# Layer 1 of tokens 0-1023: blocks 7 to 10 in seven products, GpSimd emptied, signs by parametric ReLU, running sums in PSUM, other planner margins

## The chip, the core and the metric

One Trainium2 core runs the whole program. The metric is the device time of one execution in microseconds (us), the median of the runs. PE is the matrix engine, DVE the vector engine, ACT the scalar engine, POOL is GpSimd, SP issues the DMAs.

## What is computed

```python
x = attention(q, k, v)          # 4 x 8 heads, 576 x 64; half local (32 wide), half strided (32)
x = x / rms(x) * rms_g          # 2304 tokens x 512
h = silu(x @ w_gate) * (x @ w_val)            # d_ff 1536 = 12 blocks of 128
x = h @ w_out                                 # layer 1
h = softplus(x @ w_in)                        # d_ff 2048 = 16 blocks of 128
out = h @ w_out2                              # layer 2
```

Weights come as 64-bit floats and are turned into 32-bit floats on the chip.

## The kernel before, in words

**Products.** Each operand of a product is split in a high and a low part (`split_op`, `prep_in`, `prep_out`: ACT rounds the high part, DVE subtracts it), and each product is three matmuls (`mm3`, L459). Tokens lie in chunks of 512. Chunks 0 and 1 (tokens 0-1023) are "side 0" of layer 1, the others "side 1".

**Plain and in seven products.** `plain` makes one 128 x 512 result of gate or value with 12 matmuls. A block of d_ff over two chunks has four such results, 48 matmuls. `quad` makes the same four by Strassen's scheme (Winograd's form): seven products of 6 matmuls each, 42 in all. For it the token operands B11 to B22 (tile `ob`) are joined by four sums T1 to T4 (tile `tb`, made by `combine`), the weights by four sums (`prep_in` with `sums`), and partial results are copied and added (ACT L919 and L926, DVE L923). Before the change side 0 uses `plain` in all 12 blocks; side 1 and layer 2 use `quad`.

**Output of layer 1.** For every two blocks `out1` multiplies by w_out: six matmuls into a PSUM bank, then DVE adds the bank to the running sum `xs` (L1007).

**Weights.** `decode` makes a 32-bit float from a 64-bit one: ACT scales the upper word (L392), ACT or DVE fetches the low bits (L393 or L395), DVE takes the sign in with one operation (L397) and joins with a second (L400). 74 tiles are decoded; 42 are also written back to `w_kept` for the second use.

**Order.** Nothing runs in the order it is written. `Program.add` records an operation with its engine, its estimated length and its dependencies; `Program.emit` plays it through (`Trial`), and issues on every engine in the order of that trial. It does so twice: the first pass holds the attention and the first `DEALT` = 10 blocks of side 0, whose products fill PE beside the second half of the attention (a step of the attention queue after each product); the second pass holds all that follows. Operations made by `two` may go to POOL, if DVE has over `BESIDE` = 900 ns of work at that point.

**At the seam** the second pass makes the last norms (`last_turn`: L488 to L493), blocks 10 and 11 of side 0, and, with `combine` and `build`, the operands of side 1.

Of the kernel before, what the change touches and what calls it, by code (L numbers as in the profile page):

```python
# [37 lines left out]
W1N, W2N = DFF // 128, DF2 // 128  # L38
DEALT = 10
HOMES = (4, 6, 12)  # L40
# [4 lines left out]
WARM = 9  # L45
BESIDE = 900
EXTRA = {"gh": 3, "gl": 3}
# [5 lines left out]

HOP = {"PE": 210, "DVE": 175, "ACT": 240, "POOL": 90, "SP": 60}
WINDOW = 3413
SLACK = 10
# [5 lines left out]
class Program:  # L62
# [70 lines left out]
    def hop(self, e, i):  # L133
        return 0 if e == "PE" == self.nodes[i][0] else HOP[e]


class Trial:
# [20 lines left out]
    def run(self):  # L158
# [48 lines left out]
        while len(ends) < len(new):  # L207
# [52 lines left out]
def attn_glu_softplus(  # L260
# [17 lines left out]
    def all_of(key):  # L278
        return (key, 0, 1 << 30)
# [23 lines left out]
    def table(name):  # L303
        pr.add("ACT", 1300, lambda: nc.scalar.preload_act_table_set(name), [], [all_of("table")])

# [36 lines left out]
    x_banks = [(banks.t[i], (f"bank{i}", 0, 1 << 20)) for i in (2, 3)]  # L342
    raws = ring(const, "raw", 2, [128, 512], U64)
    cvt = ring(const, "cvt", 1, [128, 512])
# [39 lines left out]
    def decode(src, t, kt, keep):  # L384

        raw, kraw = raws.next()
        u, ku = cvu.next()
        words = raw.bitcast(U32).rearrange("p (n two) -> p n two", two=2)
        wlo, whi = words[:, :, 0], words[:, :, 1]
        quarters = raw.bitcast(U16).rearrange("p (n four) -> p n four", four=4)  # L390
        dma(340, lambda: nc.sync.dma_start(out=raw, in_=src), hold, [kraw])
        act(512, lambda: nc.scalar.activation(t, whi.bitcast(F32), AF.Copy, scale=2.0 ** -112), [kraw], [kt])  # L392
        pr.add("ACT", 180 + 512 / 0.98, lambda: nc.scalar.activation(  # L393
            u, quarters[:, :, 1], AF.Identity, bias=low, scale=2.0 ** -13), [kraw, all_of("eps")], [ku], alt=(68 + 512 / 1.5,
            lambda: nc.vector.tensor_scalar(out=u, in0=wlo, scalar1=29, scalar2=None,  # L395
                                            op0=ALU.logical_shift_right)))
# [3 lines left out]
        dve(560, lambda: nc.vector.scalar_tensor_tensor(  # L400
            out=t.bitcast(U32), in0=t.bitcast(U32), scalar=3, in1=u,
            op0=ALU.logical_shift_left, op1=ALU.bitwise_or), [kt, ku], [kt])
        if keep >= 3 * AGAIN:
            dma(170, lambda: nc.sync.dma_start(out=wk[keep], in_=t), [kt], [("wk", keep, keep + 1)])
# [60 lines left out]
    def stats(c, ring_):  # L465
        lo, hi = CUTS[c], CUTS[c + 1]
        n = hi - lo
        r, kr = sview(lo, hi), ("ssq", lo, hi)
        p, kp = ring_.next()
        p = p[:, :n]  # L470
        for i, kk in enumerate((0, 2, 1, 3) if c < 2 else (0,)):
# [398 lines left out]

    def step(queue, n=1):
# [24 lines left out]
    def plain(i, row, c, ring_):  # L896

        bank = ring_.next()
        lo, hi = (A11, A12) if row == 0 else (A21, A22)
        if c == 4:  # L900
            terms = [(a, B12, k, ((2 * j + k) // 2, (2 * j + k) % 2 * 256)) for j, a in enumerate((lo, hi)) for k in (0, 1)]
        else:
            xlo, xhi = (B11, B21) if c % 2 == 0 else (B12, B22)
            terms = [(a, x, k, None) for a, x in ((lo, xlo), (hi, xhi)) for k in (0, 1)]
        n = CUTS[c + 1] - CUTS[c]
        prod(bank, i, terms, n)
        return bank[0][:, :n], bank[1]
# [83 lines left out]
    def out1(fs, g, first, c, d):  # L991
# [5 lines left out]
        for f in fs:  # L997
            i = f % 4
            mv, km = g[f, c]
            pairs.append(([wout[i][:, x, d * 128:(d + 1) * 128] for x in (0, 1)], mv,  # L1000
                          lambda a, b, i=i, km=km: [(f"wout{i}", a * 512 + d * 128, a * 512 + d * 128 + 128), km[b]]))
        mm3(pb, kp, pairs, n)
        x, kx = xview(d, lo, hi)
        if first:
# [32 lines left out]
    def combine(c0, c1, over):  # L1037

        for k in (0, 1):
# [11 lines left out]
            split_op(y, ky, T4, k, eng="DVE")  # L1051

    def build(c0, c1, c4, sums=True):

# [11 lines left out]
    def w_at(f, side):  # L1066
        return (f % 2, 0) if side else (0, f % 2 * 4)

    def prep1(f, side, parts=(0, 1)):
        src = [None] * 3 if side and f >= AGAIN else [w1[f, :, j * 512:(j + 1) * 512] for j in range(3)]  # L1070
        if 0 in parts:
            prep_in(w_at(f, side), [(3 * f, src[0]), (3 * f + 1, src[1])], side, True, "POOL")
        if 1 in parts:
            prep_out(f % 4, 3 * f + 2, src[2])
# [5 lines left out]
    def prep2(p, all4, eng):  # L1080
        i = ((W1N + p) % 2, 0)
        o = 3 * W1N + 4 * p
        prep_in(i, [(o, None), (o + 2, None)], True, all4, eng)
        for j in (0, 1):
            prep_out((2 * p + j) % 4, o + 2 * j + 1, None)
        return i

    with tc.manual_schedule():
# [29 lines left out]
        def early():  # L1118
            use.s = s_banks
            direct(0)  # L1120
            half(0, 0, f_banks)
            stats(0, v_banks)

# [48 lines left out]
        with ExitStack() as c2:  # L1172
# [3 lines left out]
            pr.side = True  # L1176
            half(1, 0, s_banks)
            pr.side = False
            table("silu_and_others")
# [13 lines left out]
            for i in (0, 1):  # L1193
# [5 lines left out]
                fk["gv"].t.append(ssq[:, i * CH:i * CH + CH])  # L1199
            queue, last_turn = steps(x, {-1: (1,), 1: (2,)}, tv)  # L1200
            step(queue, 5)
# [4 lines left out]
            prep1(DEALT, 0)  # L1206
            pr.emit()
            if RAW:
                fk["gv"].t, fk["gv"].keys = fk["gv"].t[:2], {}
                give(i for i in (0, 1) if i not in RAW)  # L1210
# [19 lines left out]
        for s, f in enumerate([*range(AGAIN, W1N), *range(AGAIN)]):  # L1230
# [15 lines left out]
            g[f, c1] = chain1(gb1, vb1)  # L1246
            for k in range(max(0, 3 * s - 6), min(3 * s - 3, 2 * W1N)):
                early2(k)
# [6 lines left out]
        for side, (c0, c1, c4) in enumerate(SIDES):  # L1255
# [97 lines left out]
```

## Time and profile before

| | |
|---|---|
| median of 3 runs | 895.45 us (894.0 to 895.78) |
| the profiled execution | 895.19 us |
| its span, first to last instruction | 893.4 us |
| PE busy | 877.4 us (98%), 5372 instructions |
| DVE busy | 699.6 us (78%), 1291 |
| ACT busy | 508.3 us (57%), 977 |
| POOL busy | 61.5 us (7%), 57 |

The busy time of an engine is the union of its instructions' durations. On DVE the duration of an instruction runs a little into that of the next one, so instructions that follow each other at once start closer than they last. Of PE's matmuls some records are missing.

### The profile page before, as it was taken

What the parts mean: (1) busy time and instruction counts of PE and PEld (TensorE: products, weight loads), DVE (VectorE), ACT (ScalarE), POOL (GpSimd) and SP (SyncE); (2) the same over time, 40 slices, a digit from 0 to 9 for tenths busy, and PEclk for the clock granted to TensorE, in tenths of its full rate; (3) what the DMA queues carried; (4) which work ended last, traced back from release to release, by engine and by line L of the source; (5) the groups of instructions that cost most, each with busy time, mean ns of one, the idle gap of its engine ahead of it and who ended that gap; (6) DMA issues with size and microseconds to landing.
All of it is one profiled execution on the core that took longest, in us unless ns stands there. A gap on an engine that the chain in (4) does not pass through costs nothing.

```text
span 893.4 us, 14068 instructions
## 1 busy us (share of the span) xinstructions
PE 877.4 (98%) x5372; PEld 726.9 (81%) x5372; DVE 699.6 (78%) x1291; ACT 508.3 (57%) x977; POOL 61.5 (7%) x57
## 2 busy tenths in 40 slices
PE   7999999999999999999999999999999999999998
PEld 6677887888877888888888888888888888888887
DVE  4999999997699976787998798867798456666545
ACT  2997766663454677464665468644474655434331
POOL 1010202110013100000100010000010000000000
PEclk7999999999999999999999999999999999999999
DMA  7765766522211454453542024511114011101003
GB/s 245 251 200 165 248 218 211 166 99 105 71 59 48 132 182 158 154 195 123 188 135 79 1 96 153 172 52 48 48 48 165 24 48 48 48 27 44 1 1 118
DMA packets 41141, 102.17 MB, mean 114 GB/s; under 512 B 4721, under 2 KB 5745, under 8 KB 41073
## 3 DMA queue, kind: packets, MB, share of 16 engines
q1 hardware_dynamic: 41072, 101.27, 35.0%
q8 instruction: 42, 0.69, 0.3%
q14 instruction: 27, 0.21, 0.1%
HBM read 80.28 MB, written 20.97 MB: 113 GB/s over the span
## 4 chain that ended last, share of the span: by engine, by line
PE 89%; DVE 6%; ACT 3%; DMA 2%; issue 1%; SPq 0%; DVEq 0%
PE bank L459 84%; PE bank L760 1%; PE bank L706 1%; PE bank L617 1%; DVE xs L1007 1%; DMA id_sb<-ident 1%; DMA w_kept<-cvtx 1%; DVE xs L376 1%; DVE tb L376 1%; DVE gv L376 0%; PE bank L483 0%; ACT eb L664 0%; PE bank L604 0%; ACT eb L668 0%; DVE gv L492 0%
## 5 line engine op out<-in xcount | busy, mean ns | idle before, releaser
L459 PE MATMUL bank<-ob,win 128*128 128x512 f32 (+1 forms) x1560 | 441.3, 360 | 1.2 <-ACT win L430 0.7
L459 PEld LDWEIGHTS bank<-ob,win 128*128 128x128 f32 x1560 | 282.6, 188 | 54.5 <-issue 2.3
L459 PE MATMUL bank<-tb,win 128*128 128x512 f32 x672 | 233.2, 392 | 1.4 <-DVE xs L1007 1.2
L459 PEld LDWEIGHTS bank<-tb,win 128*128 128x128 f32 x672 | 124.3, 188 | 24.3 <-DVE xs L1007 1.4
L1029 DVE TENSOR_TENSOR xs<-bank,xs 128x512 f32<-128x512 f32 (+1 forms) x127 | 86.8, 685 | 52.4 <-PE bank L459 51.1
L430 ACT ACTIVATE win<-w 128x512 fp32r<-128x512 f32 (+1 forms) x136 | 83.4, 615 | 54.9 <-PE bank L459 28.7
L376 DVE TENSOR_TENSOR win<-w,win 128x512 fp32r<-128x512 f32 (+1 forms) x125 | 84.3, 678 | 22.3 <-ACT win L430 19.4
L459 PE MATMUL bank<-wout,ghx 128*128 128x512 f32 x304 | 99.7, 389 | 0.0
L459 PE MATMUL bank<-wout,gh 128*128 128x512 f32 (+1 forms) x276 | 89.9, 386 | 0.0
L459 PE MATMUL bank<-ghx,wout 128*128 128x512 f32 x224 | 84.1, 393 | 0.0
L459 PE MATMUL bank<-gh,wout 128*128 128x512 f32 (+1 forms) x256 | 80.1, 353 | 1.4 <-DVE xs L1007 1.1
L1007 DVE TENSOR_TENSOR xs<-bank,xs 128x512 f32<-128x512 f32 (+1 forms) x100 | 62.4, 630 | 11.0 <-PE bank L459 9.6
L459 PEld LDWEIGHTS bank<-wout,ghx 128*128 128x128 f32 x304 | 56.9, 188 | 11.8
L459 PEld LDWEIGHTS bank<-wout,gh 128*128 128x128 f32 x276 | 51.2, 188 | 10.6
L459 PE MATMUL bank<-wout,glx 128*128 128x512 f32 x152 | 53.8, 389 | 0.0
L459 PEld LDWEIGHTS bank<-gh,wout 128*128 128x128 f32 x256 | 45.3, 189 | 10.1 <-DVE xs L1007 2.5
L459 PEld LDWEIGHTS bank<-ghx,wout 128*128 128x128 f32 x224 | 42.0, 188 | 8.4
L459 PE MATMUL bank<-wout,gl 128*128 128x512 f32 (+1 forms) x138 | 48.1, 386 | 0.0
L376 DVE TENSOR_TENSOR w<-w 128x256 f32<-128x256 f32 x110 | 46.0, 418 | 1.1
L459 PE MATMUL bank<-glx,wout 128*128 128x512 f32 x112 | 43.4, 394 | 0.0
L459 PE MATMUL bank<-gl,wout 128*128 128x512 f32 (+1 forms) x128 | 42.4, 351 | 0.0
L393 ACT ACTIVATE cvu<-raw,low 128x512 uint32<-128x512 uint16 x44 | 33.6, 763 | 11.4 <-DVE cvtx L400 4.5
(164 smaller groups left out, 1234.2 us busy)
## 6 DMA issues: line engine op xcount, KB each, us to landing
raw<-w SPq DMA_DIRECT2D x74, 512.0 KB, 3.8
w<-w_kept SPq DMA_DIRECT2D x52, 256.0 KB, 2.6
qk<-qk SPq DMA_DIRECT2D x15, 608.0 KB, 6.8
w_kept<-cvtx SPq DMA_DIRECT2D x25, 256.0 KB, 2.5
cvt<-w_kept SPq DMA_DIRECT2D x25, 256.0 KB, 2.8
w_kept<-w SPq DMA_DIRECT2D x20, 256.0 KB, 2.8
w_kept<-cvt SPq DMA_DIRECT2D x17, 256.0 KB, 2.5
cvtx<-w_kept SPq DMA_DIRECT2D x17, 256.0 KB, 2.8
```

Of the source, the lines that this page charges most:

```text
L376: pr.add("DVE", 68 + n / 0.96, lambda: getattr(nc.vector, name)(o, x, y), r, w, alt=(110 + n * 2.3, lambda: getattr(nc.gpsimd, name)(o, x, ...
L393: pr.add("ACT", 180 + 512 / 0.98, lambda: nc.scalar.activation(u, quarters[:, :, 1], AF.Identity, bias=low, scale=2.0 ** -13), [kraw, all_ ...
L430: act(n, lambda: nc.scalar.activation(h, t, AF.Copy), [kt], [reg(0, o + lo, o + hi)])
L459: lambda a=a, b=b, i=i, st=st, mv=mv: nc.tensor.matmul(o, lhsT=st[a], rhs=mv[b], start=(first and i == 0), stop=(last and i == m - 1), ski ...
L617: nc.tensor.matmul(sp[o, a * nk:(a + 1) * nk], lhsT=qt[r, c:c + 64], rhs=qt[r, QW + c:QW + c + nk], start=False, stop=True, skip_group_che ...
L706: pr.add("PE", 108, lambda a=a, a0=a0, tp=tp: nc.tensor.transpose(tp[:kp, a * 128:a * 128 + 128], pv[:, a0 + a, :], id_sb), [kpv, all_of(" ...
L760: pr.add("PE", 59 if loc else 36, lambda a=a, h=h, o=o, t=t: nc.tensor.matmul(xb[64 * h:64 * h + 64, a * nq:(a + 1) * nq], lhsT=vt[r0:r1, ...
L1007: dve(n, lambda: nc.vector.tensor_add(x, pb, x), [kp, kx], [kx])
L1029: dve(n, lambda x=x, pb=pb: nc.vector.tensor_add(x, pb, x), [kp, kx], [kx])
```

## The change

It does five things.
1. **Blocks 7 to 10 of side 0 by `quad`** (`QUADS`, `side_q`). `combine_ops` makes T1 to T4 for side 0 out of the split operands, since `xs` holds the running sums by then; `combine` for side 1 moves from block 10 to block 11. `DEALT` goes to 5, and the attention queue takes three steps at a time (`PACE`).
2. **Nothing on GpSimd** (`BESIDE` = 1e9): 51 tensor operations go from POOL to DVE. Two memsets stay.
3. **Signs by parametric ReLU**: ACT scales the upper word with another factor for negative numbers (`Prelu`, alpha -2^32), so that the sign is in the exponent and comes out of the shift; the first of the two joining operations on DVE goes.
4. **Running sums copied into PSUM** (`KEPT`): on side 0, from the second pair of blocks on, ACT copies `xs` into the bank ahead of `out1`'s matmuls, these add onto it, and the bank is copied back by ACT or DVE. 36 additions on DVE become 36 copies in on ACT and 36 copies out (23 on ACT, 13 on DVE).
5. **Margins**: in the planner a result for PE counts as 100 ns later, and a DMA's as 1600 ns later for the others. A third buffer `raw`; four more buffers `gvw`; `early2` (decoding for layer 2) all in side 1 of layer 1.

```diff
-DEALT = 10
+DEALT, QUADS = 5, (7, 11)
+PACE = 3
+KEPT = (0, 1, 2, 3)
+KEEPF = 2
-BESIDE = 900
+BESIDE = 1e9
+MARGIN, LATE = 100, 1600
+def lag(e, to):
+    if e == "PE":
+        return 0 if to == "PE" else HOP[e]
+    return HOP[e] + (MARGIN if to == "PE" else LATE if e == "SP" else 0)
...
-        act(512, lambda: nc.scalar.activation(t, whi.bitcast(F32), AF.Copy, scale=2.0 ** -112), [kraw], [kt])
+        act(512, lambda: nc.scalar.activation(t, whi.bitcast(F32), AF.Prelu, scale=2.0 ** -112, alpha=-2.0 ** 32),
+            [kraw, all_of("slope")], [kt])
+            shifted.append(nc.vector.tensor_scalar(out=u, in0=ti, scalar1=3, scalar2=None, op0=ALU.logical_shift_left))
+            a, b, n, op = (wlo, u, 29, ALU.logical_shift_right) if shifted else (ti, u, 3, ALU.logical_shift_left)
+            nc.vector.scalar_tensor_tensor(out=ti, in0=a, scalar=n, in1=b, op0=op, op1=ALU.bitwise_or)
-        dve(560, lambda: nc.vector.scalar_tensor_tensor(
-            out=u, in0=t.bitcast(U32), scalar=0x80000000, in1=u, op0=ALU.bitwise_and, op1=ALU.bitwise_or),
-            [kt, ku], [ku])
...
+        if c < 2 and d in KEPT and fs[0] >= KEEPF and kp[0] in primed:
+            act(n, lambda: nc.scalar.activation(pb, x, AF.Copy), [kx], [kp])
+            mm3(pb, kp, pairs, n, False)
+            evict(n, x, pb, [kp], [kx])
+            return
...
+    def combine_ops():
+        for k in (0, 1):
+            y = whole(B12, k)
+            t = fk["gv"].next()
+            less(t, y, parts(B11, k))
+            split_op(*t, T1, k, eng="DVE")
+            z = whole(B22, k)
+            less(y, z, [y])
+            split_op(*y, T3, k, eng="DVE")
+            less(z, z, [t])
+            split_op(*z, T2, k, eng="DVE")
+            x = whole(B21, k)
+            less(x, x, [z])
+            split_op(*x, T4, k, eng="DVE")
...
+            if f in range(*QUADS):
+                if f == QUADS[0]:
+                    drain(len(todo))
+                    o_banks.t, o_banks.keys = banks.t[4:], {}
+                side_q(f)
+                continue
             side_a(f, [None, None, (last_turn,)] if f == DEALT else [])
             if f == DEALT:
+                combine_ops()
+            if f == QUADS[1]:
                 combine(*SIDES[1][:2], False)
```

**How the order moves.** The first pass holds 1,545 matmuls and 429 operations on DVE before, 1,191 and 344 after; the program has 24 matmuls fewer in all (1,752 of 512 columns with `ob` or `tb` before, 1,728 after).

DVE, just behind the seam, before (`gv` and `tb`: sums for side 1; L1007: additions of `out1`; L397 and L400: a decode):

```order
L1007 TENSOR_TENSOR xs<-bank_76,xs 128x512
L376 TENSOR_TENSOR gv_84<-xs,gv_85 128x512
L376 TENSOR_TENSOR tb<-gv_85,tb 128x512
L1007 TENSOR_TENSOR xs<-bank_73,xs 128x512
L971 TENSOR_TENSOR gv_85<-bank_77,ssq 128x512
L1007 TENSOR_TENSOR xs<-bank_74,xs 128x512
L397 SCALAR_TENSOR_TENSOR cvu_82<-cvtx,cvu_82 128x512
L974 TENSOR_TENSOR gv_85<-bank_78,gv_85 128x512
L400 SCALAR_TENSOR_TENSOR cvtx<-cvtx,cvu_82 128x512
```

and with the change, where the seam lies five blocks earlier (`ob`, `gvw`, `gv`: `combine_ops`; L1032 is the addition, L409 and L413 the decode):

```order
L387 TENSOR_TENSOR gvw_2011<-gvw_2011,gvw_2010 128x512
L1032 TENSOR_TENSOR xs<-bank_76,xs 128x512
L387 TENSOR_TENSOR gvw_2012<-gvw_2012,gvw_2011 128x512
L989 TENSOR_TENSOR gv_85<-bank_77,ssq 128x512
L387 TENSOR_TENSOR tb<-gvw_2011,tb 128x512
L1032 TENSOR_TENSOR xs<-bank_73,xs 128x512
L413 SCALAR_TENSOR_TENSOR cvt_82<-cvt_82,cvu_83 128x512
L1032 TENSOR_TENSOR xs<-bank_74,xs 128x512
L992 TENSOR_TENSOR gv_85<-bank_78,gv_85 128x512
L413 SCALAR_TENSOR_TENSOR w_84<-w_84,cvu_83 128x512
L387 TENSOR_TENSOR tb<-gv_86,tb 128x512
L409 TENSOR_SCALAR cvu_83<-w_84 128x512
```

The sums for `tb` now stand among the work of blocks 5 and 6, not of 10 and 11, and a decode has one joining operation.

PE, in front of the first `quad`, before (side 1; `ob` 128x256 are the products of chunk 4):

```order
L459 MATMUL bank_74<-ghx_101,wout_99 128x512
L459 MATMUL bank_71<-ob,win_90 128x512
L459 MATMUL bank_75<-ob,win_90 128x256 x5
L459 MATMUL bank_76<-ob,win_90 128x256 x3
L459 MATMUL bank_74<-tb,win_90 128x512 x2
L459 MATMUL bank_71<-tb,win_90 128x512
L459 MATMUL bank_74<-tb,win_90 128x512
```

and with the change (block 7 of side 0; `gh`, `gl` by `wout` are `out1` of blocks 4 and 5):

```order
L475 MATMUL bank_74<-gh_88,wout_98 128x512
L475 MATMUL bank_74<-gl_90,wout_98 128x512
L475 MATMUL bank_74<-gh_88,wout_98 128x512
L475 MATMUL bank_72<-ob,win_91 128x512
L475 MATMUL bank_71<-tb,win_2003 128x512 x5
L475 MATMUL bank_74<-tb,win_2003 128x512 x2
L475 MATMUL bank_71<-tb,win_2003 128x512
L475 MATMUL bank_74<-tb,win_2003 128x512 x2
```

The first product with `tb` is the 172nd matmul of the second pass; the blocks 5 and 6 stand between the seam and it.

## Rows read from the trace of the kernel before

**Rows 1.** The page, parts 1 and 2: engines' totals, DVE's busy tenths in 40 slices.
```profile
PE 877.4 (98%) x5372; PEld 726.9 (81%) x5372; DVE 699.6 (78%) x1291; ACT 508.3 (57%) x977; POOL 61.5 (7%) x57
...
DVE  4999999997699976787998798867798456666545
```

**Rows 2.** The chain that ended last, share of the span by engine.
```profile
PE 89%; DVE 6%; ACT 3%; DMA 2%; issue 1%; SPq 0%; DVEq 0%
```

**Rows 3.** Stretches: us, then PE, PEld, DVE, ACT, POOL busy (instructions), clock, DMA.
```profile
0.00:20.00 20.00, 14.66 (x231) 12.50 (x235) 7.03 (x25) 3.95 (x9) 2.34 (x7) 0.74 0.73 233
20.00:60.00 40.00, 36.12 (x599) 27.08 (x596) 37.46 (x107) 37.34 (x130) 4.27 (x6) 1.00 0.75 250
60.00:200.00 140.00, 139.51 (x1187) 111.66 (x1179) 132.08 (x261) 98.67 (x177) 23.37 (x21) 1.00 0.57 182
200.00:240.00 40.00, 40.00 (x251) 32.54 (x250) 25.09 (x42) 14.49 (x28) 0.00 (x0) 1.00 0.22 70
240.00:300.00 60.00, 57.72 (x262) 46.40 (x261) 59.03 (x100) 33.32 (x57) 12.82 (x10) 1.00 0.22 69
300.00:520.00 220.00, 219.62 (x1153) 188.32 (x1152) 181.59 (x326) 134.08 (x237) 11.49 (x9) 1.00 0.41 134
520.00:880.00 360.00, 359.80 (x1674) 300.19 (x1673) 251.03 (x428) 186.44 (x344) 7.16 (x4) 1.00 0.20 63
```

**Rows 4.** Waits for others, PEld, 238 to 300 us; timeline of PE (start, us).
```profile
PEld bank L459 <- DVE xs L1007: 4.0, 5, 1.4
...
285.95 1.42 PE L459 MATMUL bank<-tb,win 128*128 128x512 f32 x5 [1.21 <-DVE xs L1007]
```

**Rows 5.** Timeline of PE in layer 2: matmuls that follow each other at once.
```profile
600.32 0.39 PE L459 MATMUL bank<-tb,win 128*128 128x512 f32 x1
600.54 0.39 PE L459 MATMUL bank<-wout,gh 128*128 128x512 f32 x1
600.77 0.39 PE L459 MATMUL bank<-tb,win 128*128 128x512 f32 x1
```

**Rows 6.** Timeline of DVE: two at once; first of the second pass.
```profile
256.64 0.68 DVE L376 TENSOR_TENSOR gv<-xs 128x512 f32<-128x512 f32 x1
257.24 0.68 DVE L376 TENSOR_TENSOR xs<-xs,ssq_b 128x512 f32<-128x512 f32 x1
...
238.11 0.69 DVE L397 SCALAR_TENSOR_TENSOR cvu<-w,cvu 128x512 uint32<-128x512 uint32 x1 [0.51 <-ACT w L392]
```

**Rows 7.** Groups by form: the decode (count, busy us, mean ns, idle before).
```profile
L397 DVE SCALAR_TENSOR_TENSOR cvu<-w,cvu 128x512 uint32<-128x512 uint32 x28 | 19.1, 682 | 2.8 <-ACT w L392 1.4 <-ACT cvu L393 1.2
...
L392 ACT ACTIVATE w<-raw 128x512 f32<-128x512 f32 x28 | 18.5, 672 | 8.4 <-DMA raw<-w 4.0 <-DVE mz L632 2.9 <-DVE win L376 1.3
```

**Rows 8.** Groups by form: work of a quad and of `out1`.
```profile
L926 ACT ACTIVATE bank<-bank 128x512 f32<-128x512 f32 x28 | 16.4, 584 | 12.2 <-PE bank L459 10.4 <-DVE xs L1007 1.4
L919 ACT ACTIVATE gv<-bank 128x512 f32<-128x512 f32 x28 | 16.7, 597 | 24.3 <-PE bank L459 24.2
L376 DVE TENSOR_TENSOR w<-w 128x256 f32<-128x256 f32 x110 | 46.0, 418 | 1.1
L1007 DVE TENSOR_TENSOR xs<-bank,xs 128x512 f32<-128x512 f32 x80 | 54.3, 683 | 8.8 <-PE bank L459 7.7
```

**Rows 9.** GpSimd's largest group; a DVE group slowed beside it; both in the timeline.
```profile
L377 POOL TENSOR_TENSOR win<-w,win 128x512 fp32r<-128x512 f32 x11 | 15.0, 1368 | 117.2 <-PE bank L459 101.2 <-DVE cvt L400 13.0 <-ACT win L430 3.1
...
L376 DVE TENSOR_TENSOR xs<-xs,ssq_b 128x512 f32<-128x512 f32 x6 | 5.6, 946 | 0.0
...
249.45 1.41 POOL L377 TENSOR_TENSOR xs<-xs,ssq_b 128x512 f32<-128x512 f32 x1 [56.48 <-DVE ssq_b L493]
250.83 1.73 POOL L377 TENSOR_TENSOR win<-w,win 128x512 fp32r<-128x512 f32 x1
...
250.23 2.88 DVE L376 TENSOR_TENSOR xs<-xs,ssq_b 128x512 f32<-128x512 f32 x2
```

**Rows 10.** Waits of PEld with no visible releaser, 60 to 238 us.
```profile
PEld bank L760 <- issue: 2.6, 9, 0.4
```

More of the change, by code (lines that the diff above doesn't have):

```diff
@@ L303, in table @@
     def table(name):
-        pr.add("ACT", 1300, lambda: nc.scalar.preload_act_table_set(name), [], [all_of("table")])
+        pr.add("ACT", 1300, lambda: nc.scalar.preload_act_table_set(name), [], [all_of("table")] + [all_of("slope")] * (name == "softplus"))
     class Ring:
@@ L869, in steps, with step @@
         return out, lambda: turn((), (3, 4))
-    def step(queue, n=1):
+    def step(queue, n=PACE):
         for _ in range(min(n, len(queue))):
@@ L905, in plain @@
         n = CUTS[c + 1] - CUTS[c]
+        (primed.add if n == CH else primed.discard)(bank[1][0])
         prod(bank, i, terms, n)
@@ L1001, in out1 @@
                           lambda a, b, i=i, km=km: [(f"wout{i}", a * 512 + d * 128, a * 512 + d * 128 + 128), km[b]]))
+        x, kx = xview(d, lo, hi)
+        if c < 2 and d in KEPT and fs[0] >= KEEPF and kp[0] in primed:
[3 more added lines that the diff above has]
+            return
         mm3(pb, kp, pairs, n)
-        x, kx = xview(d, lo, hi)
+        if n == CH:
+            primed.add(kp[0])
         if first:
@@ L1051, in combine, with parts, whole, less @@
             split_op(y, ky, T4, k, eng="DVE")
+    def combine_ops():
+        def parts(slot, k):
+            return list(zip([x.bitcast(F32) for x in op_of(slot, k)[0]], op_of(slot, k)[1]))
+        def whole(slot, k):
+            (h, kh), (l, kl) = parts(slot, k)
+            o, ko = fk["gv"].next()
+            two("DVE", CH, "tensor_add", o, h, l, [kh, kl], [ko])
+            return o, ko
+        def less(o, x, ys):
+            for y, ky in ys:
+                sub("DVE", CH, o[0], x[0], y, [x[1], ky], [o[1]])
+                x = o
+        for k in (0, 1):
[11 more added lines that the diff above has]
+            split_op(*x, T4, k, eng="DVE")
     def build(c0, c1, c4, sums=True):
@@ L1066, in w_at @@
     def w_at(f, side):
-        return (f % 2, 0) if side else (0, f % 2 * 4)
+        if side:
+            return ((f + 1) % 2, 0)
+        return ((f - QUADS[0] + 1) % 2, 0) if f in range(*QUADS) else (0, f % 2 * 4)
     def prep1(f, side, parts=(0, 1)):
+        sums = side or f in range(*QUADS)
         src = [None] * 3 if side and f >= AGAIN else [w1[f, :, j * 512:(j + 1) * 512] for j in range(3)]
         if 0 in parts:
-            prep_in(w_at(f, side), [(3 * f, src[0]), (3 * f + 1, src[1])], side, True, "POOL")
+            prep_in(w_at(f, side), [(3 * f, src[0]), (3 * f + 1, src[1])], sums, side or not sums, "POOL")
         if 1 in parts:
@@ L1119, in early @@
             use.s = s_banks
+            if 0 not in RAW:
+                stats(0, v_banks)
             direct(0)
             half(0, 0, f_banks)
-            stats(0, v_banks)
+            if 0 in RAW:
+                stats(0, v_banks)
         def prepare(f, parts, u):
@@ L1177, in attn_glu_softplus @@
             half(1, 0, s_banks)
+            if 1 not in RAW:
+                stats(1, v_banks)
             pr.side = False
@@ L1199, in attn_glu_softplus @@
                 fk["gv"].t.append(ssq[:, i * CH:i * CH + CH])
-            queue, last_turn = steps(x, {-1: (1,), 1: (2,)}, tv)
+            queue, last_turn = steps(x, {-1: tuple(c for c in RAW if c), 1: (2,)}, tv)
             step(queue, 5)
@@ L1246, in attn_glu_softplus @@
             g[f, c1] = chain1(gb1, vb1)
-            for k in range(max(0, 3 * s - 6), min(3 * s - 3, 2 * W1N)):
+            for k in range(max(0, 3 * s - 3), min(3 * s, 2 * W2N)):
                 early2(k)
```

50 lines of the change are left out of this document (34 added, 16 removed).

## The prediction

> **What bounds the kernel now.** I read the totals first [rows 1]: PE is busy 877.4 us of the span of 893.4, DVE 699.6, ACT 508.3. A busy PE can still be a waiting one, so the chain of waits is next [rows 2]: 89% of it is PE, 6% DVE. Then the table of stretches [rows 3], which shows where the 6% lies. From 300 us on PE idles 0.38 us in 220 and 0.20 in 360, and each matmul starts 0.225 us after the one before it [rows 5]: there only fewer matmuls help. In the first 60 us the attention is held by DMA, DVE and ACT. From 60 to 200 us DVE is at 132.08 of 140 (94%) and PE hardly idles; from 200 to 240 DVE has air (25.09 of 40). From 240 to 300, around the seam, DVE is full (59.03 of 60) and PE idles 2.28 us. The waits there go to DVE, to the additions of `out1` [rows 4]. So PE is the bound, and DVE stands right behind it for most of the first 300 us. What the change does to DVE there decides what of the saved matmuls is seen.
>
> **The sum** is made against the profiled execution, 895.19 us (span 893.4 and 1.8 around it). The median of the runs, 895.45, is 0.26 higher, which I add at the end.
>
> *Matmuls.* Four blocks at 48 - 42 = 6 matmuls fewer are 24. At 0.225 us [rows 5] that is **-5.4 us**. PE is the bound on both sides of the place, so I count all of it.
>
> *Work of the other engines over the whole program.* On DVE one operation of 128x512 follows another after 0.60 us [rows 6], though each lasts 0.68; for 128x256 I take 0.42 - 0.08 = 0.34 [rows 8]. DVE loses 74 sign operations (their duration: [rows 7]), 74 x 0.60 = 44 us, and 36 - 13 = 23 additions or copies of running sums, 14 us. It gains 24 operations of `combine_ops`, 14 us; 8 additions of quads, 5 us; 16 weight sums, 5 us, and 8 more splits, 4 us; and GpSimd's 51 operations, some 25 us at DVE's spacing (27 are 128x512). Net about -5 us. ACT gains 59 copies for the running sums at 0.58 to 0.60 [rows 8], 35 us, and 15 us of quads and sums: from 508 to some 560 of 893. I cost ACT's gain at nothing, since it stays under two thirds; the cover is PE's own work, and where a copy comes late the product that it opens waits (second rival). Prelu is not in the trace: between the price of the scaling copy, 0.672 [rows 7], and nothing less; 0.1 us more on each of 74 would be 7 us of an engine with 330 us to spare. I take 0.672.
>
> *GpSimd's shadow.* A DVE operation that meets one on POOL takes longer: a pair of `xs` by `ssq_b` took 2.88 us at 250.23, when POOL was at work from 249.45 to 252.56, against 0.68 for a single one later, and the group of six means 946 ns against 683 for the additions [rows 6, 8, 9]. That goes. The rule on the other side is the Trainium skill's, "Perfetto Trace Analysis", Optimizing Scalar/DVE Operations: when DVE is saturated, handing work to the scalar engine or even GpSimd may make sense, though the two share a read port. By its first half, taking 51 operations off POOL where DVE is at 94% would put up to 25 us back on the bound behind PE; by the stretched rows much of that is returned. I side with the rows.
>
> *The seam of before.* With the sums for side 1 spread out, and the additions [rows 4] turned into copies, I let PE's 2.28 us of idle time go: **-2.3 us** (bounds 0 and -2.3). At the new side change the order has all splits for side 1 within about 112 us of DVE work from the seam, where PE has some 118.
>
> *The new hot place.* The attention's second half and five blocks now lie in one shorter pass. Before, the first pass ended at about 238 us [rows 6]; 354 matmuls fewer x 0.225 = 80 us, so PE can be through at 158. DVE's work of that pass, summed over its order at the spacing above, falls from about 193 to 136 us. In the first 20 us DVE gets 7 done [rows 3], so 129 us must fit in 138: 93%, against 85% before. Right behind, blocks 5 and 6 give PE 171 matmuls = 39 us before the first product with `tb`, and the order has 39 us of DVE work in the same piece. Together: 168 us of DVE work in 177 us of PE. How full can DVE be? From 60 to 200 us its work by the same count was 127 us in 140, 91%; at that rate it needs 185 us and PE waits 8 us. From 240 to 300 it was 54 in 60, but the pair at 250.23 alone lost 1.6 us [rows 9], and I count 4.5 us of such stretching there; without it 97%, that is 173 us, no wait at all. The upper rate is nearer, since POOL is gone; also the last T1 split stands 18 us of DVE work behind the seam and is needed after 39. Single late results remain: **+2.0 us** (bounds 0 and 8).
>
> *Changes of form on PE.* In the first pass the groups of attention and block matmuls go from 125 to 132. The dearest such gaps are 2.6 / 9 = 0.29 us [rows 10], most cost next to nothing: **+0.3** (0 to 2.0).
>
> *Start, DMA, margins.* The order of the first 60 us stays nearly the same on PE, and DVE reaches block 0's second weight split after 26.6 us of work, not 25.4: 0, with 2 us either way. DMAs are off the chain but for 2% [rows 2]; the margins alter the order alone, and `early2` moves within a stretch in which DVE is at 181.59 of 220 and PE idles 0.38. SP's queue gets no DMA more. If that cover fails, a weight split would be late next.
>
> Sum: 895.19 - 5.4 - 2.3 + 2.0 + 0.3 = 889.8; with 0.26 on top, **890.0 us**.
>
> **Rivals.** *The seam is cured altogether* (17%): DVE gets so much air that no wait remains: 895.45 - 7.7 = 887.8, less with a better start. For it: DVE has 5 us less to do and no shadow. A rule of the Trainium skill points this way, "SBUF — State Buffer", Who interferes with whom: a DVE operation with two SBUF inputs and a GpSimd operation that reads SBUF exclude each other for a whole instruction. By it GpSimd's 61 us could each have stood in DVE's way; the group of `w` sums at 418 ns and most others at 0.68 [rows 8, 6] show that few did.
>
> *The copies into PSUM show* (17%): a bank can take its next sum only when ACT has copied it in, where before the matmuls began at once. If a fifth of 36 x 0.58 us shows, 4.3 us come on: 894.3, no change to measure. For it: ACT is an in-order queue with decodes and quad copies ahead of these; before, ACT L926 waited 10.4 us for PE [rows 8]. Against it: four banks, and other products to run between.
>
> *DVE becomes the bound* (14%): it keeps the 91% of 60 to 200 us. Then 895.45 - 5.4 - 2.3 + 8.2 + 2.0 = 898.0, slower. The place is 100 to 200 us, and it decides from a DVE rate of about 90%: the new waits must pass 7.7 us, plus the 1.8 of the measurement, or half of it with a seam that stays. For it speaks that this is the only rate the trace shows over a long stretch; against it, that PE was served on time there, so nothing forced more.
>
> *It does not do what it says*: the copies need a bank whose last group covered it, and the order shows 36 of 40 sums treated so; the quads stand there. It gets no chance.
>
> **Numbers.** About 0.2% (1.8 us) can be told from no change. Forecast 52% at 890.0, rivals 17, 17 and 14. Faster by over 0.2%: forecast, first rival and a part of the second, 0.72; within: 0.15; slower: 0.13. The range goes from 885.5 (first rival with 2 us of a better start) to 897.0 (second rival with a stubborn seam, and most of the third left out).
>
> **What would show it.** PE's matmuls 24 fewer, POOL at two memsets, no DVE group above 0.75 us for 128x512, a decode with one joining row; ACT near 560 us busy, DVE near 690. Seam at 157 to 162 us, and there a DVE at 57 or more of 60 with PE idle about 2 us; from 300 us on the same spacing of 0.225. I am wrong if PE idles over 8 us between 100 and 210, if waits for the ACT copies lead PE's list, or if the gain lies in the first 60 us.

## The result, and the profile after

The changed kernel takes 884.74 us (median of 4 runs, 882.61 to 886.43) against 894.99 (894.0 to 895.78) for the kernel before: a ratio of 0.9895 with a 95% interval of 0.9877 to 0.9913, some 10 us faster. The forecast was 890.0 us in a range of 885.5 to 897.0: the sign was right, and the gain is nearly twice the one forecast (10.25 us against 5.45). As a time, 884.74 lies 0.8 us below the lower end of the range; as a ratio, 0.9895 of the 895.45 that the forecast started from is some 886, just inside it. The profiled execution took 882.61 us, its span is 880.8.

The page's parts 1 and 2 (engines' totals; DVE's busy tenths and PE's granted clock in 40 slices) and part 4 (the chain that ended last):

```profile
PE 870.1 (99%) x5348; PEld 724.9 (82%) x5348; DVE 684.0 (78%) x1308; ACT 548.9 (62%) x1057; POOL 1.6 (0%) x6
...
DVE  5999999999999767787779976778797366666545
...
PEclk8999999999999999999999999999999999999999
...
PE 94%; DVE 2%; DMA 1%; ACT 1%; issue 0%; SPq 0%; ACTq 0%
```

Against [rows 1] PE has 24 matmuls fewer, POOL has nothing but memsets left, ACT has 41 us more and DVE 16 us less. Against [rows 2] the chain has 94% PE in place of 89%, and 2% DVE in place of 6%. PE's granted clock is below full only in the first 60 us.

The same stretches as in [rows 3] (us, then PE, PEld, DVE, ACT, POOL busy, with instructions in brackets; granted clock, DMA), and PE's own list of waits from 60 to 300 us, which is complete (the weight loads have a list of their own; the waits for the additions of `out1`, 4.0 us in [rows 4], are gone from it):

```profile
0.00:20.00 20.00, 16.25 (x298) 13.73 (x300) 9.35 (x33) 5.53 (x18) 1.62 (x6) 0.83 0.83 270
20.00:60.00 40.00, 36.90 (x519) 28.19 (x514) 36.41 (x106) 37.20 (x121) 0.00 (x0) 0.96 0.75 256
60.00:200.00 140.00, 139.53 (x1266) 111.50 (x1266) 137.05 (x287) 115.48 (x212) 0.00 (x0) 1.00 0.50 162
200.00:240.00 40.00, 40.00 (x178) 33.15 (x177) 38.36 (x71) 34.30 (x63) 0.00 (x0) 1.00 0.48 145
240.00:300.00 60.00, 60.00 (x292) 50.73 (x291) 54.94 (x98) 47.96 (x91) 0.00 (x0) 1.00 0.36 117
```

```profile
PE bank L500 <- DVE ssq_b L387: 0.3, 1, 0.3
PE bank L475 <- ACT ghx L976: 0.2, 1, 0.2
```

The hot place has come where it was forecast, and DVE is fuller there than it was: 137.05 of 140 us, 97.9%, against 132.08. Yet PE idles 0.47 us in these 140, and not at all from 200 to 300.

The groups by form that answer to [rows 7 to 9] (count, busy us, mean ns, idle before): the decode's scaling (L404) and its only joining operation (L413), the new copies into PSUM (L1022), a DVE group that was slowed beside GpSimd, and the additions of `out1`:

```profile
L404 ACT ACTIVATE w<-raw 128x512 f32<-128x512 f32 x28 | 18.9, 684 | 1.2 <-DVE win L387 1.1
L1022 ACT ACTIVATE bank<-xs 128x512 f32<-128x512 f32 x36 | 21.4, 597 | 2.7 <-DVE xs L302 1.6 <-DVE xs L1032 0.8
...
L413 DVE SCALAR_TENSOR_TENSOR w<-w,cvu 128x512 uint32<-128x512 uint32 x15 | 10.3, 687 | 1.1 <-ACT cvu L415 0.9
L387 DVE TENSOR_TENSOR xs<-xs,ssq_b 128x512 f32<-128x512 f32 x8 | 5.6, 695 | 0.0
L1032 DVE TENSOR_TENSOR xs<-bank,xs 128x512 f32<-128x512 f32 x44 | 30.1, 689 | 10.6 <-PE bank L475 10.3
```

The parametric ReLU costs 684 ns where the copy cost 672 [rows 7] (in the two other groups 668 and 670 ns against 666 and 670); `xs` by `ssq_b` has fallen from a mean of 946 ns [rows 9] to 695; 36 of the 80 full-width additions are gone.

### The profile page after: what moved, and what is told of

It is laid out like the page before. It is cut to its first block, busy times and chain, and to the rows that moved or that the text cites. A ratio compares the mean times of both kernels' runs of the same rounds, so it can differ in the third digit from the quotient of the medians.

```text
span 880.8 us, 13995 instructions
## 1 busy us (share of the span) xinstructions
PE 870.1 (99%) x5348; PEld 724.9 (82%) x5348; DVE 684.0 (78%) x1308; ACT 548.9 (62%) x1057; POOL 1.6 (0%) x6
## 4 chain that ended last, share of the span: by engine, by line
PE 94%; DVE 2%; DMA 1%; ACT 1%; issue 0%; SPq 0%; ACTq 0%
PE bank L475 90%; PE bank L723 1%; PE bank L777 1%; PE bank L634 1%; DMA id_sb<-ident 1%; PE bank L500 1%; DMA qk<-qk 1%; DVE mz L649 0%; PE bank L621 0%; DVE ssq_b L387 0%; ACT eb L681 0%; ACT xs L305 0%; ACT pt L305 0%; DVE pp L387 0%; DVE xs L303 0%
## 5 line engine op out<-in xcount | busy, mean ns | idle before, releaser
L475 PE MATMUL bank<-ob,win 128*128 128x512 f32 (+1 forms) x1440 | 396.3, 357 | 0.5 <-ACT win L446 0.3
L475 PEld LDWEIGHTS bank<-ob,win 128*128 128x128 f32 x1440 | 258.1, 189 | 46.3 <-issue 1.9
L475 PE MATMUL bank<-tb,win 128*128 128x512 f32 x768 | 253.2, 391 | 0.0
L475 PEld LDWEIGHTS bank<-tb,win 128*128 128x128 f32 x768 | 142.7, 188 | 26.3
L1054 DVE TENSOR_TENSOR xs<-bank,xs 128x512 f32<-128x512 f32 (+1 forms) x127 | 87.0, 687 | 46.4 <-PE bank L475 44.6
L387 DVE TENSOR_TENSOR win<-w,win 128x512 fp32r<-128x512 f32 (+1 forms) x144 | 95.0, 664 | 23.0 <-ACT win L446 14.8
L446 ACT ACTIVATE win<-w 128x512 fp32r<-128x512 f32 (+1 forms) x144 | 87.2, 609 | 39.0 <-DVE w L387 21.1
L387 DVE TENSOR_TENSOR w<-w 128x256 f32<-128x256 f32 x128 | 53.8, 420 | 0.8
L1032 DVE TENSOR_TENSOR xs<-bank,xs 128x512 f32<-128x512 f32 (+1 forms) x64 | 38.5, 606 | 12.4 <-PE bank L475 11.7
L1006 ACT ACTIVATE raw<-bank 128x512 f32<-128x512 f32 (+1 forms) x48 | 25.3, 527 | 29.0 <-PE bank L475 28.0
```

The costliest lines, as they stand in the source:

```text
L387: pr.add("DVE", 68 + n / 0.96, lambda: getattr(nc.vector, name)(o, x, y), r, w, alt=(110 + n * 2.3, lambda: getattr(nc.gpsimd, name)(o, x, ...
L446: act(n, lambda: nc.scalar.activation(h, t, AF.Copy), [kt], [reg(0, o + lo, o + hi)])
L475: lambda a=a, b=b, i=i, st=st, mv=mv: nc.tensor.matmul(o, lhsT=st[a], rhs=mv[b], start=(first and i == 0), stop=(last and i == m - 1), ski ...
L1006: act(n, lambda: nc.scalar.activation(l, h, AF.Softplus), [kp], [kl], True)
L1032: dve(n, lambda: nc.vector.tensor_add(x, pb, x), [kp, kx], [kx])
L1054: dve(n, lambda x=x, pb=pb: nc.vector.tensor_add(x, pb, x), [kp, kx], [kx])
```

## The experiments

Two theories stand behind them. **A**, the prediction's: PE is the bound, a matmul less is 0.225 us less, and of DVE's work only what comes late shows. **B**: the gain comes from DVE (room, or no more shadow of GpSimd), and the saved matmuls are partly paid back. The kernels whose names begin with u, v and w are the changed one with an edit, c is the changed one as it is; those with p are the kernel before with one part of the change or more. The changed kernel's 8 runs in two sets have their median at 884.3, and the differences below are to that.

### The quads

**u1_no_quads**: side 0 all in plain products again.

```diff
-DEALT, QUADS = 5, (7, 11)
+DEALT, QUADS = 5, (11, 11)
...
-            if f == DEALT:
+            if f == DEALT and QUADS[0] < QUADS[1]:
                 combine_ops()
```

> The changed kernel with blocks 7 to 10 of tokens 0-1023 in eight plain products again: 24 matmuls more on PE, and by the order some 24 us less work on DVE and 20 us less on ACT; all else stays. Theory A (PE is the bound, each matmul shows at 0.225 us, and DVE's extra work lies under PE's): 884.7 + 5.4 = 890.1 us, between 889 and 891.5. Rival B (DVE binds in the first 240 us, and the quads only move the wait): with 24 us less on DVE the waits go, and 24 matmuls more are half paid back: 885 to 887.5. Rival C (the banks that the quads take cost the running sums time): under 889 as well, with less PE idle time around blocks 7 to 10.

Measured: 887.43 us (6 runs, 886.24 to 891.17; ratio to before 0.9931, 0.9912 to 0.995), 3.1 us above the changed kernel. That looks as if half of the 5.4 were paid back: it lies where Rival B put it (885 to 887.5), not where Theory A did. The trace speaks against B. Up to the end of the attention both kernels have the same matmuls, 1,883 of them before the last `ssq_b` product. Timelines of PE (start, us), the changed kernel first, then u1_no_quads:

```profile
7.16 1.04 PE L634 MATMUL bank<-qk 64*64 64x96 f32 x34 [1.31 <-DMA qk<-qk]
...
157.28 0.59 PE L500 MATMUL bank<-ssq_b,ones 128*128 128x256 f32 x2
```

```profile
6.13 1.04 PE L634 MATMUL bank<-qk 64*64 64x96 f32 x34 [0.15 <-DMA qk<-qk]
...
155.51 0.59 PE L500 MATMUL bank<-ssq_b,ones 128*128 128x256 f32 x2
```

From that product to the end of the span it is 880.8 - 157.28 = 723.5 us with the quads and 884.5 - 155.51 = 729.0 without: 5.5 us for 24 matmuls, 0.228 each (the spans are given to 0.1 us, so 5.4 is as good a reading). Ahead of it the two differ by the start: in this execution of u1_no_quads q and k landed a microsecond earlier, and it reached the same product 1.8 us sooner. The quads have no part in that: DVE and ACT run the same operations in the same order in both kernels up to 153 us. PE's list of waits from 60 to 300 us has the same two rows in both, which speaks against Rival C. Theory A holds for the quads behind this product; the medians carry the start as well, in which the 6 executions of u1_no_quads may have been luckier (only one of them has a trace).

**c_after_again**: the changed kernel without an edit.

> The changed kernel once more, without any edit, for more executions of it. In the runs so far one kernel's time goes with the mean granted clock of the run: blocks in plain products gave 886.2 us at 1.0, 888.0 at 0.994 and 891.1 at 0.992. Theory, the start's clock makes this spread: the same here, about 881 to 883 at 0.996 and above, 883 to 885 at 0.994, 885 to 887 at 0.992; at an equal clock it then lies 4.5 to 5.5 us below the kernel with plain products, as 24 matmuls x 0.225 would have it. Rival, the quads pay only half: 2 to 3.5 us below it at an equal clock.

Measured: 884.08 us (4 runs, 882.76 to 886.06), with the mean granted clock from 0.996 (882.8 and 883.9) to 0.992 (886.1). At 0.992 it lies 5.0 us below u1_no_quads (886.06 and 891.1), at 0.994 3.7 (884.22 and 887.95): nearer to theory A, by few runs. The trace says more:

```profile
157.42 0.59 PE L500 MATMUL bank<-ssq_b,ones 128*128 128x256 f32 x2
```

881.0 - 157.42 = 723.6 us, as in the first trace of this kernel. What differs between executions of this kernel lies before this product.

**w_warm_start**: five more dummy matmuls at the start, to hold the clock. In the changed kernel's trace the granted clock is 0.5 (1.2 of 2.4 GHz) from 9 to 15 us; in that of u1_no_quads it is 1.0 there.

```diff
+        def warm(n):
+            for _ in range(n):
+                nc.tensor.matmul(f_banks.t[0][:, :128], lhsT=ones, rhs=ones, start=True, stop=True)
...
-            pr.add("PE", 400, lambda: nc.tensor.matmul(
-                f_banks.t[0][:, :128], lhsT=ones, rhs=ones, start=True, stop=True), [all_of("ones")], [("bank6", 0, 128)])
+            pr.add("PE", 400, lambda i=i: warm(6 if i == WARM - 1 else 1), [all_of("ones")], [("bank6", 0, 128)])
```

> The changed kernel with five more dummy matmuls of 128 columns ahead of the first mask product, where PE then waits 1.3 us for the first q and k; the order of all else is the same. Theory, the drop of the granted clock to 0.5 from 8.3 to 15.7 us follows the thin activity before it: the clock stays at 1.0 or drops for a shorter time, and 1.5 to 3.5 us go, 881 to 883, with less spread between executions. Rival, the drop stays, or the start is held by DMA anyway: 884 to 886.

Measured: 883.18 us (6 runs, 880.48 to 887.85; ratio 0.9882, 0.9861 to 0.9902). The clock kept to 1.0 in the first 20 us of the profiled execution, and then fell for a while twice, to 0.91 as a mean of 20 to 40 and of 40 to 60 us:

```profile
0.00:20.00 20.00, 17.29 (x346) 15.15 (x349) 10.88 (x37) 7.23 (x28) 1.61 (x6) 1.00 0.90 280
20.00:40.00 20.00, 16.00 (x240) 11.58 (x239) 16.47 (x48) 15.21 (x50) 0.00 (x0) 0.91 0.80 252
```

PE did more in the first 20 us (17.29 against 16.25) and less in the next 20 (16.00). The intervals overlap, the spread is no smaller, and the theory of this run, that the clock alone makes the spread, does not hold: one execution at 0.996 took 887.85. The last `ssq_b` product starts at 158.66 here, and 882.2 - 158.66 = 723.5 us follow: a third execution with the same time behind it. Which part of the spread is the clock and which the landing of q and k stays open.

**v1_quads_from_6**: one more block in seven products.

```diff
-DEALT, QUADS = 5, (7, 11)
+DEALT, QUADS = 5, (6, 11)
```

> The changed kernel with the quads from block 6 on, five blocks in place of four: 6 matmuls fewer, some 7 us more on DVE, and the sums of the tokens' operands are needed some 18 us earlier, in the stretch where DVE is at 97% and more. Theory, DVE has no air left there: the splits come late and PE waits 2 to 8 us for them, 885 to 891. Rival, the planner puts other work off: the 6 matmuls show, 1.35 us less, 882.5 to 884.

Measured: 884.15 us (4 runs; ratio 0.989, 0.9873 to 0.9906), no better. It lies between the two expectations, and the trace shows both at work. The first row of PE's waits from 60 to 300 us, and the stretch of the first quad:

```profile
PE bank L475 <- ACT ghx L976: 0.8, 2, 0.6
```

```profile
180.00:200.00 20.00, 19.36 (x83) 15.20 (x83) 19.71 (x38) 16.52 (x31) 0.00 (x0) 1.00 0.46 149
```

Six matmuls fewer are 1.35 us; PE now idles 0.64 us here and starts 83 matmuls in 20 us, where the changed kernel starts 90. From the last `ssq_b` product (157.18 us) to the end it takes 723.9 us, 0.3 more than the changed kernel, where six matmuls fewer alone would give 1.35 less. The air that the four quads left is used up.

### GpSimd

**u2_gpsimd_back** and **p1_before_no_gpsimd**: the same edit, in the changed kernel and backwards in the kernel before.

```diff
-BESIDE = 1e9
+BESIDE = 900
```

> The changed kernel with GpSimd given work again by the planner's old rule: by the order 47 operations, some 23 us, go to POOL and 18 us leave DVE; the matmuls stay. Theory of the shadow (DVE operations beside POOL's are stretched): 128x512 groups of DVE beside POOL rise above 0.72 us and 1.5 to 5 us come back: 886.5 to 890. Rival, air for DVE (18 us less on an engine that is at 97% or more from 60 to 200 us): 882 to 884. No effect, since PE never waits for either: 884 to 885.5.

> The kernel before, with only its work on GpSimd forbidden (one of the change's parts alone): by the order 52 operations leave POOL and 50, some 21 us, come to DVE. Theory of the shadow: stretched DVE operations go, and with them waits around the seam: 3 to 7 us less, 888 to 892. Rival, DVE has no air (94% from 60 to 200 us, 98% from 240 to 300): 2 to 8 us more, 897 to 903.

Measured: 891.92 us (5 runs; ratio 0.9969, 0.9957 to 0.9981) with GpSimd put back, 7.6 more than the changed kernel and more than any theory gave; 890.77 us (6 runs; ratio 0.9963, 0.9949 to 0.9976) with GpSimd taken from the kernel before, 3.6 less. Though DVE gets 50 operations more in the kernel before (its busy time rises from 699.6 to 710.7 us), the time falls. In u2_gpsimd_back the last `ssq_b` product starts 5.8 us later than in the changed kernel, though its start was not slower:

```profile
163.10 0.59 PE L500 MATMUL bank<-ssq_b,ones 128*128 128x256 f32 x2
```

So 5.8 of some 7.9 us between the two profiled executions are lost in the attention with the dealt blocks, and some 2 behind it.

How a GpSimd operation costs PE time is seen best in the trace of a run told below, p2_before_prelu. Timelines of DVE, POOL and PE (start, us):

```profile
160.39 0.68 DVE L376 TENSOR_TENSOR win<-w,win 128x512 fp32r<-128x512 f32 x1
160.99 1.77 DVE L376 TENSOR_TENSOR wout<-cvtx,wout 128x512 fp32r<-128x512 f32 x1
162.69 1.78 DVE L376 TENSOR_TENSOR xs<-xs,ssq_b 128x512 f32<-128x512 f32 x1
164.39 0.54 DVE L291 COPY pt<-bank 96x384 f32<-96x384 f32 x1
164.86 0.67 DVE L979 TENSOR_TENSOR gvx<-bank,gvx 128x512 f32<-128x512 f32 x1
...
160.59 3.32 POOL L377 TENSOR_TENSOR xs<-xs,ssq_b 128x512 f32<-128x512 f32 x2 [3.68 <-issue]
...
165.58 0.50 PE L464 MATMUL bank<-ob,win 128*128 128x512 f32 x1 [1.36 <-DVE gvx L979]
```

Two DVE operations of the 0.68 us kind last 1.77 and 1.78 us beside POOL's pair; `gvx`, two places behind them, is 2.2 us late, and PE idles 1.36 us for it. The Trainium skill's "SBUF — State Buffer", Who interferes with whom, says that a DVE instruction with two SBUF inputs contends with a GpSimd instruction that reads SBUF. The trace agrees: both stretched operations have two SBUF inputs. It also shows that not every such operation is stretched: `win`, of the same kind, starts 0.2 us ahead of POOL's pair and keeps its 0.68. The other sentence that the prediction draws on (the Trainium skill's "Perfetto Trace Analysis", Optimizing Scalar/DVE Operations), that handing work to GpSimd may make sense when DVE is saturated, came out the other way here in both kernels: taking it back from GpSimd gave 3.6 and 7.6 us. The same passage warns that moving work between those two might not help.

### The decoding

**u3_old_decode**: the changed kernel with the two joining operations.

```diff
-        act(512, lambda: nc.scalar.activation(t, whi.bitcast(F32), AF.Prelu, scale=2.0 ** -112, alpha=-2.0 ** 32),
-            [kraw, all_of("slope")], [kt])
+        act(512, lambda: nc.scalar.activation(t, whi.bitcast(F32), AF.Copy, scale=2.0 ** -112), [kraw], [kt])
...
+        dve(560, lambda: nc.vector.scalar_tensor_tensor(
+            out=u, in0=t.bitcast(U32), scalar=0x80000000, in1=u, op0=ALU.bitwise_and, op1=ALU.bitwise_or),
+            [kt, ku], [ku])
```

> The changed kernel with the old decoding (scaling copy, then two joining operations on DVE for the sign and the low bits): 58 DVE operations more, some 34 us in all, about 12 us of them in the first 200 us, where DVE is busy 97% and more. Theory, the parametric ReLU makes the room in which the quads hide: 8 to 14 us more, 893 to 899. Rival, DVE's time from 60 to 200 us is partly early work that can be put off: 0 to 3 us more, 885 to 888.

Measured: 898.86 us (5 runs; ratio 1.0046, 1.0033 to 1.0059), 14.6 more, and slower than the kernel before. The two stretches in which DVE is full, and PE's last `ssq_b` product:

```profile
60.00:200.00 140.00, 138.04 (x1257) 108.01 (x1256) 135.12 (x288) 109.52 (x200) 0.00 (x0) 0.99 0.45 149
200.00:300.00 100.00, 98.92 (x442) 79.75 (x441) 98.17 (x178) 81.16 (x151) 0.00 (x0) 1.00 0.34 111
```

```profile
165.41 0.59 PE L495 MATMUL bank<-ssq_b,ones 128*128 128x256 f32 x2
```

The attention ends 8.1 us later than in the changed kernel, DVE stays full until 300 us (98.17 of 100), and PE now idles there too. Part of this may be the granted clock, 0.97 as a mean of 100 to 160 us, where the changed kernel's is 1.00; the runs do not separate it. Without the new decoding the other parts together lose more than they win. Half of the loss lies ahead of the first quad, so it is not the quads alone that need the room.

**p2_before_prelu**: the kernel before with the new decoding alone (the edit above the other way round).

> The kernel before, with only the new decoding (the sign by parametric ReLU, one joining operation on DVE): by the order 51 operations, some 36 us, leave DVE; GpSimd keeps 48 of its operations. Theory, room on DVE cures the seam and the hot stretch: 4 to 8 us less, 887 to 891. Rival, the shadow stays and PE waits as before: 0 to 2 us less, 893 to 895.

Measured: 900.69 us (6 runs; ratio 1.007, 1.005 to 1.009), 6.3 more than before: neither theory. **p3_prelu_no_gpsimd** has `BESIDE = 1e9` besides.

> The kernel before with two parts of the change together: the new decoding, and nothing on GpSimd. By the order DVE has 20 operations and some 23 us less than in the kernel before, POOL 52 less. Alone, GpSimd off gave 3.6 us less and the new decoding 6.3 us more. Theory, the new decoding lost its time to stretched operations of DVE beside POOL (in its trace DVE's operations beside POOL cost 16 us more than alone, and one such pair held PE for 1.36 us at 164 us): with POOL empty the room shows, 886 to 889.5. Rival, it lost by an order planned too tight, in which results come late by the planner's own account: 892 to 897.

Measured: 900.67 us (4 runs; ratio 1.0075, 1.0058 to 1.0092). The same time, but not the same loss. The stretch from 60 to 200 us, p2_before_prelu first, then this run:

```profile
60.00:200.00 140.00, 135.45 (x1167) 106.28 (x1167) 116.79 (x227) 92.57 (x164) 24.90 (x22) 1.00 0.58 179
60.00:200.00 140.00, 139.34 (x1150) 111.08 (x1151) 122.68 (x253) 99.83 (x178) 0.00 (x0) 1.00 0.57 183
```

PE idles 4.55 us there beside GpSimd and 0.66 without it, so the theory of the shadow fits this part (4.0 us of p2_before_prelu's waits there go to DVE). Behind the seam the time is lost again: from the last `ssq_b` product to the end this run takes 654.2 us, p2_before_prelu 650.1 and p1_before_no_gpsimd, with the old decoding, 644.4. In this run's trace: the groups of ACT's table loads; the last stretch; PE's largest wait from 516 to 600 us; and a piece of ACT's timeline.

```profile
L304 ACT ACT_TABLE_LOAD x13 | 16.7, 1283 | 0.9 <-PEq L1346 0.7
L393 ACT ACT_TABLE_LOAD x7 | 9.0, 1283 | 0.1
L993 ACT ACT_TABLE_LOAD x7 | 9.0, 1283 | 0.1
```

```profile
520.00:880.00 360.00, 353.50 (x1632) 293.44 (x1631) 238.78 (x409) 200.06 (x350) 0.00 (x0) 1.00 0.20 63
```

```profile
PE bank L464 <- ACT ssq L924: 4.3, 3, 2.3
```

```profile
557.26 1.28 ACT L993 ACT_TABLE_LOAD   x1
558.56 0.60 ACT L993 ACTIVATE raw<-bank 128x512 f32<-128x512 f32 x1
559.18 1.28 ACT L393 ACT_TABLE_LOAD   x1
560.47 0.66 ACT L393 ACTIVATE cvtx<-raw 128x512 f32<-128x512 f32 x1
```

The decoding (L393) and the softplus (L993) change ACT's table back and forth: the kernel before decodes its last 8 tiles in layer 2, between the softplus activations. A copy needs no other table; the parametric ReLU does: 14 loads more here, and 8 more in p2_before_prelu, where the 8 decodings stand in four groups. The Trainium skill's "ScalarE: Activation LUTs", What ACT_TABLE_LOAD costs, gives 1.283 us for a load and 1.38 us of draining for each switch; the trace agrees with the first, and shows no second (ACT's idle time ahead of these groups is 0.1 us). The changed kernel has all these decodings in layer 1, and 13 table loads.

**p4_prelu_early_decodes**: p3_prelu_no_gpsimd with that move.

```diff
-            for k in range(max(0, 3 * s - 6), min(3 * s - 3, 2 * W1N)):
+            for k in range(max(0, 3 * s - 3), min(3 * s, 2 * W2N)):
                 early2(k)
...
-                if side == 0 and p < 4:
-                    early2(2 * W1N + 2 * p)
-                    early2(2 * W1N + 2 * p + 1)
```

> The kernel before with three parts of the change: nothing on GpSimd, the new decoding, and the last 8 early decodings of layer 2's weights moved ahead of the switch to the softplus table (as the change has them). The runs with the new decoding but without that move show 8 and 14 more table loads on ACT, of 1.28 us each, all between 516 and 580 us, where PE waits for ACT and the last stretch (from 520 us) is 3.4 and 10.2 us longer than in the kernels without. Theory, these loads are what the new decoding lost: 13 loads as before, the stretch back, 889 to 891.5, which is the time of GpSimd off alone (890.8); the new decoding by itself then gives nothing, since without the quads PE does not wait for DVE's work. Rival A, with the loads gone the relief of DVE shows as well: 886 to 889. Rival B, the loss lies elsewhere: 895 to 901.

Measured: 889.83 us (7 runs; ratio 0.9961, 0.9945 to 0.9977), 10.8 less than without the move. That is the theory's time; Rival B is out, and Rival A's range is missed by 0.8 us, which the noise allows. PE's stretch is whole again. It is so, too, in p1_before_no_gpsimd (second row), which decodes the same 8 tiles in layer 2 with the scaling copy: the cost lies in the table loads, not in the place.

```profile
520.00:880.00 360.00, 360.00 (x1676) 301.05 (x1675) 240.57 (x410) 180.53 (x331) 0.00 (x0) 1.00 0.16 50
520.00:880.00 360.00, 360.00 (x1677) 300.89 (x1676) 249.52 (x425) 182.53 (x336) 0.00 (x0) 1.00 0.21 67
```

And the new decoding by itself gives a microsecond at most, less than the runs can tell (890.77 without it): room on DVE is worth little in the old order, and 14.6 us in the new one. Which part of the new order needs it, the quads or the shorter first pass, no run separates.

### Running sums and margins

**u4_no_running_sums** (`KEPT = ()`) and **u5_no_margins** (`MARGIN, LATE = 0, 0`).

> The changed kernel with no running sum copied into PSUM: each block pair's product is added by DVE as before. By the order 14 operations and 8 us more on DVE, 50 operations and 30 us less on ACT. Theory, the copies are hidden and relieve DVE: 1 to 4 us more, 886 to 889. Rival, the copies delay the product that they open (the second rival of the prediction): 1 to 4 us less, 881 to 884.

> The changed kernel with the planner's two margins (0.1 us for a result that PE takes, 1.6 us for a transfer) at zero; the work of each engine is the same to 2 operations. Theory, the margins keep late results off PE: 1.5 to 5 us more, 886 to 889, as waits of PE of under 1 us each between 60 and 240 us. Rival, with DVE off the bound they do nothing: 883 to 885.5, and the last 3,100 products take 637.2 us as in the changed kernel, within 0.3.

Measured: 884.88 us (6 runs; ratio 0.9891, 0.9872 to 0.9909) without the running sums, so neither theory: they neither help nor hurt by more than the runs can tell. 886.25 us (4 runs; ratio 0.9912, 0.9897 to 0.9926) without the margins, 1.9 more, as its theory gave at its lower end, though the intervals overlap and part of it may be the start. The place is the stretch that was expected:

```profile
100.00:160.00 60.00, 58.78 (x565) 45.78 (x564) 57.46 (x121) 49.94 (x91) 0.00 (x0) 1.00 0.46 153
```

```profile
PE bank L500 <- DVE ssq_b L387: 1.0, 1, 1.0
```

PE idles 1.22 us here (0.27 in the changed kernel), nearly all in one wait of 1.0.

No kernel tried beats the changed one by more than the runs can tell.

## Why the prediction was right, and too small

- **Matmuls, -5.4**: right. 5.4 to 5.5 by the landmark above.
- **The seam, -2.3: mis-sized.** The step read PE's idle time, which is only a lower bound: a matmul lasts 0.39 us and the next can start after 0.225 [rows 5], so one that starts up to 0.16 late leaves no idle time and makes the busy time longer. Counting starts over the same work tells more. The last 3,104 matmuls of the kernel before and of u1_no_quads have the same widths, 457 of 512 and 145 of 256 columns in the first 602, 2,011 and 491 in the rest. (The trace of the kernel before has all 1,752 matmuls of 512 columns with `ob` or `tb` that the program has, so missing records do not blur this.) Windows (us, PE busy with its matmuls, clock), before first, then u1_no_quads, p1_before_no_gpsimd and p4_prelu_early_decodes:

```profile
247.54:372.29 124.75, 122.47 (x602) 1.00 0.35 115
372.29:893.40 521.11, 517.06 (x2502) 1.00 0.26 83
```

```profile
243.72:364.74 121.02, 121.02 (x602) 1.00 0.40 131
364.74:884.50 519.76, 516.34 (x2502) 1.00 0.24 76
```

```profile
244.26:367.02 122.76, 121.79 (x602) 1.00 0.34 108
367.02:886.90 519.88, 516.38 (x2502) 1.00 0.26 85
```

```profile
249.83:370.85 121.02, 121.02 (x602) 1.00 0.36 118
370.85:891.30 520.45, 516.90 (x2502) 1.00 0.26 83
```

  The first 602 take 3.7 us less in u1_no_quads, 2.3 of it idle time and 1.4 busy time; the rest take 1.4 less. That is 5.1 in place of 2.3. GpSimd's absence alone gives 2.0 and 1.2 of it, and with the new decoding besides the first 602 take the same 121.0 us as in u1_no_quads. So the seam was cured by these two; the step's reason, the sums spread out and the additions turned into copies, was not needed, as p4_prelu_early_decodes has neither. What gives the last 0.7 us behind is not separated. The first rival ("cured altogether", 17%) described this; it too was priced by the idle time.
- **The new hot place, +2.0, and forms, +0.3: did not come.** PE idles 0.47 us from 60 to 200, and by the sum below the kernel loses nothing ahead of the landmark. Of the two rates that the prediction had for DVE, 91% and 97%, the upper one held, for the reason it gave (POOL gone): with GpSimd back PE waits again, and the kernel takes 891.9.
- **The start, 0**: not an effect of the change that can be shown. The profiled executions differ there (in the one of before q and k came later, as the 54-column products start at 10.54 us against 9.18), and the 8 executions of the changed kernel lie 3.8 us apart, the 6 of u1_no_quads 4.9.
- **Sum.** Between the two profiled executions 12.6 us lie: 5.5 matmuls, 5.1 seam and behind, 1.4 at the start, some 0.6 in the rest ahead of the landmark. The medians differ by 10.3: the 1.4 and 0.6, in which the start's luck is, make most of the difference to 12.6.
- **The move of `early2`, 0**: right as a time, wrong as a reason. It was costed as work under PE's cover; it is what lets the parametric ReLU cost no table loads, worth 10.8 us in p4_prelu_early_decodes.
- **Rivals.** The copies into PSUM (17%) show nothing: no wait on PE's list goes to L1022 (one weight load waited 0.2 us for it), and without them the time is the same within the noise. DVE as the bound (14%) did not come, but it was near: u3_old_decode and v1_quads_from_6 show that the air is used up.

## What to carry to other kernels

Size a stall by matmul starts between the same two products, not by PE's idle time; and compare two kernels from a landmark behind the start, where executions of one kernel scatter. Two kernels with the same time may have lost it in two places: compare them stretch by stretch before a cause is ruled out. Before an activation function is replaced by another, look at which tables stand around each place where it runs: the price may lie hundreds of microseconds from the gain. Room on an engine that is nearly the bound may be worth little by itself and much in an order that fills it: the decoding gave a microsecond at most in the old order and 14.6 us in the new one.

## What the runs showed of the hardware

- PE was fed with 0.47 us of idle time by a DVE busy for 97.9% of 140 us, with GpSimd empty.
- The parametric ReLU with a slope of its own took 668 to 684 ns for 128x512, a scaling copy 666 to 672; between softplus activations it took a table load of 1283 ns, and the next softplus another (14 loads for 8 uses, two of which stood side by side).
- Behind the last product of the attention, two executions of the changed kernel took 723.5 and 723.6 us, and one with more dummy matmuls at the start 723.5: the scatter between these executions lies ahead of it.
